# Front items of the expert stage: their tables, gathers and weight loads put some steps sooner and in the other order, and small tiles resized

## The chip, the cores and the metric

The kernel runs on one core of one Trainium2 chip. The metric is the time of one execution on the device in microseconds (us). Before the change it is 1503.58 us, the median of 3 runs (1500.83 to 1508.85).

## What is computed

Three stages in a row, all in float32. N = 4608 tokens (8 batches of 576), 512 channels (8 heads of 64).

```python
kv  = einsum('bhsd,bhse->bhde', k, v); o = einsum('bhsd,bhde->bhse', q, kv)
x   = o / sqrt(mean(o*o, -1) + 1e-6) * g_norm          # attention, (4608, 512)

logits = x @ w_gate + modality_bias[modality_id]       # 8 experts
e_idx  = argmax(logits); gate_w = softmax(logits)[e_idx]
x[mask_e] = gate_w * (relu(x[mask_e] @ w1[e]) @ w2[e]) # w1 512x1024, w2 1024x512

gate = sigmoid(x @ w_gate2); val = x @ w_val2          # 512 -> 1536
out  = (gate * val) @ w_out2                           # 1536 -> 512
```

With the inputs drawn, the experts 0 to 7 get 895, 331, 414, 770, 426, 483, 718 and 571 tokens; of the first half of the tokens they get 442, 187, 206, 364, 209, 236, 367 and 293.

## The kernel before

Precision comes from splitting each float32 operand into a high and a low part (suffix h and l): a product is three matmuls, high by high, high by low, low by high. ACT makes the high part, DVE the low part.

**Attention** is a loop over batches `for b in range(B + 1)` (line 638) with five steps r = 0 to 4 in each, one 128-token tile to a step; the output tile of batch b - 1 is made while batch b is prepared. DVE and POOL also route the tokens there: `norm` (L490 to L504) makes a batch's norms and logits, `choose` (L514 to L518) the expert, `rank` (L525 to L544) the token's place among its expert's, `lanes` (L551) and `numbers` (L561, L563) the tables that turn a place back into a token number. The order of each engine's instructions is the order of the code; no scheduler changes it.

**The expert stage** works on items. An item is a pair of 128-token tiles of one expert (late items a single tile). It has four steps; a step (t, j) multiplies by a quarter of w1 (`emit_B`, L266 to L268), applies relu and splits (`emit_h`, L280, L281), then multiplies by a quarter of w2 (`emit_D`, L313 to L315). Weights are loaded raw by SP (`load_w`, L190) in pieces of 512 KB, eight to an item, and split by ACT (L227) and DVE (L228). There are two raw buffers: half0, on the right of the memory, for the front items and the even items after them, and w1r1 with w2r1 for the odd ones. A piece is loaded under a flag: where the item's expert is that of the item before it in the same buffer, the transfer is skipped.

**Front items** 0 and 1 come from the first half of the tokens alone, which are routed while attention still runs. `front_items` (L579 to L604) sums the counts (matmul `tote`, L581) and chooses the two; `front_rows` (L606 to L617) makes their gather indices (`se` L611, matmuls `phe` L615, `gidx0` L617); POOL gathers their rows by indirect DMA (L208), SP reads their experts into registers (`read_item`, L167, L168), `norm_x` (L237) scales the rows and `emit_A` transposes (L245) and splits them (xh L249, xl L250). During the eight front steps the second half's routing is finished (`experts` L793 to L800, `places` L803 to L818). The front writes its result through `front.y` (`front_y`, L629) to y_d in memory.

**Items 2 to 21** run in `run`. Between their steps the third stage's weights are decoded from 64-bit floats (`Decode`: load L128, exponent on ACT L134, words and finish on DVE L140 to L149, store L155 to L157); the table `at` (L1024) says in which step s which unit is loaded, and exponent, words, finish and store come 2, 2, 3 and 4 steps after. `store_gate` (L1041, L1042) writes the gate values to memory for a later gather, `gate_t`, made in `number` (L894 to L898).

**The third stage** (GLU) follows: per step three matmuls by three (`gv`, L970 to L972), whose moving operand lies in half0, w1r1, w2r1 or other tiles and whose stationary one in a `wt` tile, and the output product (`ac`, L1335 to L1337; `wos` by `gh` and `gl`).

The change also touches the pool `oid` (bufs=3), from which `gate_t` comes. Tiles that are allocated after it lie behind it in memory.

Of the kernel before, what the change touches and what calls it, by code (L numbers as in the profile page):

```python
# [84 lines left out]
def attention_moe_glu_kernel(  # L85
# [249 lines left out]
    with ExitStack() as st:  # L335
# [243 lines left out]
        def front_items():  # L579
# [5 lines left out]
            ep = sm.tile([128, 4], F32, tag="ep", name="ep", bufs=1)  # L585
# [9 lines left out]
            nc.vector.tensor_tensor(out=le, in0=cue[3][:, 4:12].unsqueeze(1).broadcast_to(bc), in1=iota[:, 0:2].unsqueeze(2).broadcast_to(bc), op=ALU.is_le)  # L595
            nc.vector.tensor_reduce(out=ep[:, 0:2], in_=le, op=ALU.add, axis=AX)
            nc.vector.tensor_tensor(out=ep[:, 2:3], in0=ep[:, 1:2], in1=ep[:, 0:1], op=ALU.subtract)
# [3 lines left out]
            nc.vector.tensor_tensor(out=cd[:, 1:2], in0=cd[:, 1:2], in1=ep[:, 3:4], op=ALU.add)  # L601
# [25 lines left out]
        def front_y(i):  # L627
            if i == 0:
                front.y = wk.tile([128, 2, YW], F32, tag="qc", name="y", bufs=1)  # L629
            return front.y[:, i]  # L630
# [7 lines left out]
        for b in range(B + 1):  # L638
# [6 lines left out]
            for r in range(5):  # L645
                if b == B and r == 0:
                    ld_scope.close()
                    mw = [mw_scope.enter_context(tc.tile_pool(name="m_wr0", bufs=1, side="right", reuse_waits="tile"))]
                    w1p = w1_scope.enter_context(tc.tile_pool(name="m_w1", bufs=3, side="right", reuse_waits="tile"))
                    half0 = mw[0].tile([128, 2, KC * F1], F32, tag="half0", name="half0")  # L650
                    w1r.append(half0[:, 0].rearrange("p (c f) -> p c f", f=F1))
                    w2r.append(half0[:, 1].rearrange("p (c f) -> p c f", f=DM))
                    for j in range(NJ1):
                        load_w(0, j, 0)
                        load_w(0, j, 1)
                if b < B and r == 0:
                    nc.scalar.activation(out=qc[:, 1], in_=q_t[b][:, :, 1, :], func=ACTF.Copy)
                    for i in (2, 3):
                        nc.gpsimd.tensor_copy(out=qc[:, i], in_=q_t[b][:, :, i, :])
                if b:  # L660
                    emit_out(b - 1, r)
                if b < B:
                    if r == 0:
                        emit_RT(b)
                    if r < 4:
                        emit_qT((b, r), qc[:, r].rearrange("p h d -> p (h d)"))
                    elif b % 2:
                        emit_qT((b, 4), qr_t[b // 2].rearrange("p h d -> p (h d)"))
                    if r == 2:
                        emit_M(b)  # L670
                if r == 1:
                    load_kv(b + 2)
                    load_q(b + 2)
                    if b == 0:
                        load_mod()
                    if b > 1:
                        norm(b - 2)
                    for i in {5: (1,), 6: (0, 3, 2), 7: (4,)}.get(b, ()):
                        store_x(i)
                if b % 2 and b > 1:  # L680
                    if r == 3:
                        choose(b // 2 - 1)
                elif b > 2:
                    if r == 1:
                        lane = rank(b // 2 - 2)
                    elif r == 3:
                        lo = lanes(b // 2 - 2, lane)
                        if b < B:
                            numbers(b // 2 - 2, lo, False)
                if b == B - 2 and r == 2:  # L690
                    front_items()
                if b == B - 1:
                    if r == 2:
                        front_rows()
                    if r == 3:
                        for t in range(NFRONT):
                            gather(t)
                    if r == 4:
                        for t in range(NFRONT):
                            read_item(t)  # L700
                if b == B:
                    if r in (1, 2):
                        norm_x(0, r - 1)
                    if r in (2, 3):
                        emit_A(0, r - 2)
                    if r == 3:
# [85 lines left out]
        def experts():  # L792
# [4 lines left out]
            nc.vector.memset(esf[:, NITEM:NITEM + NFRONT + 2], 1.0)  # L797
            nc.vector.tensor_tensor(out=esf[:, NITEM + NFRONT + 2:2 * NITEM], in0=esf[:, NFRONT + 2:NITEM], in1=esf[:, NFRONT:NITEM - 2], op=ALU.not_equal)
# [91 lines left out]
    def number(b, i, src):  # L890
# [5 lines left out]
        if i == 0:  # L896
            gate_t[b] = oidp.tile([128, 2 * HT], F32, tag="gate", name="gate_t")
# [109 lines left out]
    with ExitStack() as st:  # L1007
# [498 lines left out]
```

## Time and profile before

| | us |
|---|---|
| median of 3 runs | 1503.58 |
| the profiled execution | 1505.5 |
| its span, first to last instruction | 1503.7 |
| PE busy in it | 1448.7 (96%) |
| DVE busy | 910.0 (61%) |
| ACT busy | 638.9 (42%) |
| POOL busy | 220.1 (15%) |
| mean granted TensorE clock, share of full | 0.987 |

PE is TensorE's matmuls, PEld its weight loads, DVE VectorE, ACT ScalarE, POOL GpSimd, SP the engine whose queue issues most transfers (SPq). In the page's 40 slices each digit is a share in tenths (9 is 90% or more). A wait is idle time of an engine, put down to what ended it. A matmul's duration overlaps the next one's, so busy time is not the sum of the durations.

### The profile page before, as it was taken

What the parts mean: (1) busy time and instruction counts of PE and PEld (TensorE: products, weight loads), DVE (VectorE), ACT (ScalarE), POOL (GpSimd) and SP (SyncE); (2) the same over time, 40 slices, a digit from 0 to 9 for tenths busy, and PEclk for the clock granted to TensorE, in tenths of its full rate; (3) what the DMA queues carried; (4) which work ended last, traced back from release to release, by engine and by line L of the source; (5) the groups of instructions that cost most, each with busy time, mean ns of one, the idle gap of its engine ahead of it and who ended that gap; (6) DMA issues with size and microseconds to landing.
All of it is one profiled execution on the core that took longest, in us unless ns stands there. A gap on an engine that the chain in (4) does not pass through costs nothing.

```text
span 1503.7 us, 22996 instructions
## 1 busy us (share of the span) xinstructions
PE 1448.7 (96%) x8670; PEld 1231.6 (82%) x8670; DVE 910.0 (61%) x1425; ACT 638.9 (42%) x1005; POOL 220.1 (15%) x304
## 2 busy tenths in 40 slices
PE   6986998999999999999999999999999999999997
PEld 6886887999999998778888887888888888888886
DVE  2566867888888887646866675343643436444342
ACT  3655644655555555745433342232322223221221
POOL 1012121222222212311011101020010200101001
PEclk9997999999999999999999999999999999999999
DMA  9984699988886757869886666556464654646444
GB/s 297 344 300 154 228 317 292 312 291 285 293 288 207 260 175 218 302 231 337 312 324 244 244 222 245 196 202 240 156 261 179 218 224 172 240 163 234 175 156 161
DMA packets 165154, 364.68 MB, mean 243 GB/s; under 512 B 21040, under 2 KB 82736, under 8 KB 157872
## 3 DMA queue, kind: packets, MB, share of 16 engines
q1 hardware_dynamic: 153104, 329.62, 63.4%
q0 software_dynamic: 10432, 32.08, 5.8%
q8 instruction: 70, 1.15, 0.3%
q10 hardware_dynamic: 1504, 1.48, 0.3%
q14 instruction: 44, 0.36, 0.1%
HBM read 302.88 MB, written 68.63 MB: 247 GB/s over the span
## 4 chain that ended last, share of the span: by engine, by line
PE 54%; DMA 4%; SPq 0%; issue 0%; POOL 0%; DVE 0%; ACT 0%; POOLq 0%; ACTq 0%
PE gv L970 10%; PE gv L972 10%; PE gv L971 10%; PE ac L1337 6%; PE ac L1335 6%; PE ac L1336 6%; DMA xg<-x_d,gidx 3%; PE gv L944 1%; PE gv L946 1%; PE gv L945 1%; PE tr L907 1%; DMA rows<-w_d 1%; DMA w_d<-d_f 0%; DMA y_d<-y,sidx 0%; SPq L1345 0%
## 5 line engine op out<-in xcount | busy, mean ns | idle before, releaser
L266 PE MATMUL ph<-xh,w1h 128*128 128x256 f32 x576 | 167.5, 291 | 5.6 <-ACT w1h L227 4.7
L974 DVE TENSOR_TENSOR gm<-u,gv 128x512 f32<-128x512 f32 x96 | 65.9, 686 | 176.4 <-PE gv L972 175.3
L267 PE MATMUL ph<-xh,w1l 128*128 128x256 f32 x576 | 165.8, 288 | 6.4 <-DVE w1l L228 6.4
L1337 PE MATMUL ac<-wos,gl 128*128 128x512 f32 x432 | 169.5, 392 | 0.0
L1335 PE MATMUL ac<-wos,gh 128*128 128x512 f32 x432 | 169.4, 392 | 0.0
L1336 PE MATMUL ac<-wos,gh 128*128 128x512 f32 x432 | 169.1, 391 | 0.0
L268 PE MATMUL ph<-xl,w1h 128*128 128x256 f32 x576 | 164.7, 286 | 0.4 <-DVE xl L250 0.4
L994 ACT ACTIVATE s<-gv 128x512 f32<-128x512 f32 x48 | 28.7, 599 | 268.7 <-issue 209.5
L267 PEld LDWEIGHTS ph<-xh,w1l 128*128 128x128 f32 x576 | 110.7, 192 | 9.5 <-DVE w1l L228 8.4
L266 PEld LDWEIGHTS ph<-xh,w1h 128*128 128x128 f32 x576 | 110.7, 192 | 8.2 <-ACT w1h L227 5.6
L970 PE MATMUL gv<-half,wt 128*128 128x512 f32 x288 | 114.3, 397 | 0.6 <-DVE u L974 0.6
L972 PE MATMUL gv<-half,wt 128*128 128x512 f32 x288 | 113.7, 395 | 0.0
L971 PE MATMUL gv<-half,wt 128*128 128x512 f32 x288 | 113.6, 394 | 0.0
L268 PEld LDWEIGHTS ph<-xl,w1h 128*128 128x128 f32 x576 | 110.8, 192 | 0.6 <-DVE xl L250 0.6
L313 PE MATMUL py<-w2h,hh 128*128 128x512 f32 x272 | 107.0, 393 | 0.0
L315 PE MATMUL py<-w2h,hl 128*128 128x512 f32 x272 | 106.7, 392 | 0.0
L314 PE MATMUL py<-w2l,hh 128*128 128x512 f32 x272 | 106.5, 392 | 0.0
L974 DVE TENSOR_TENSOR s<-u,gv 128x512 f32<-128x512 f32 x48 | 33.0, 688 | 121.2 <-PE gv L972 121.1
L1319 POOL DMA_INDIRECT out_dram<-ot,to x36 | 37.2, 1034 | 443.3 <-DVE ot L1316 191.6
L1337 PEld LDWEIGHTS ac<-wos,gl 128*128 128x128 f32 x432 | 81.1, 188 | 18.6 <-DVE gl L1304 0.4
L1336 PEld LDWEIGHTS ac<-wos,gh 128*128 128x128 f32 x432 | 81.1, 188 | 18.2
L1335 PEld LDWEIGHTS ac<-wos,gh 128*128 128x128 f32 x432 | 81.1, 188 | 18.2 <-ACT gh L1303 0.2
(305 smaller groups left out, 3370.3 us busy)
## 6 DMA issues: line engine op xcount, KB each, us to landing
wt<-wt_d SPq DMA_DIRECT2D x36, 1536.0 KB
half<-in_moe_w_dram SPq DMA_DIRECT2D x96, 512.0 KB
wos<-wo_d SPq DMA_DIRECT2D x96, 512.0 KB
w1r<-in_moe_w_dram SPq DMA_DIRECT2D x40, 512.0 KB
w2r<-in_moe_w_dram SPq DMA_DIRECT2D x40, 512.0 KB
rows<-w_d SPq DMA_DIRECT2D x24, 512.0 KB
wt<-wt_d SPq DMA_DIRECT2D x48, 256.0 KB
wt_d<-wt SPq DMA_DIRECT2D x12, 1024.0 KB
```

What stands on the lines that cost most here:

```text
L266: nc.tensor.matmul(out=o, lhsT=bh[:, c, cs], rhs=hi[:, c, 0:n], start=(c == 0), stop=False)
L267: nc.tensor.matmul(out=o, lhsT=bl[:, c, cs], rhs=hi[:, c, 0:n], start=False, stop=False)
L268: nc.tensor.matmul(out=o, lhsT=bh[:, c, cs], rhs=lo[:, c, 0:n], start=False, stop=(c == KC - 1))
L313: nc.tensor.matmul(out=o, lhsT=hi[:, f, cs], rhs=bh[:, f, :], start=first, stop=False)
L314: nc.tensor.matmul(out=o, lhsT=hi[:, f, cs], rhs=bl[:, f, :], start=False, stop=False)
L315: nc.tensor.matmul(out=o, lhsT=lo[:, f, cs], rhs=bh[:, f, :], start=False, stop=last)
L970: nc.tensor.matmul(out=o, lhsT=wh, rhs=yh[:, c, :], start=first and c == 0, stop=False, skip_group_check=True)
L971: nc.tensor.matmul(out=o, lhsT=wh, rhs=yl[:, c, :], start=False, stop=False, skip_group_check=True)
L972: nc.tensor.matmul(out=o, lhsT=wl, rhs=yh[:, c, :], start=False, stop=last and c == 1, skip_group_check=True)
L1335: nc.tensor.matmul(out=o, lhsT=gh[:, cs], rhs=wh, start=(k == 0), stop=False)
L1336: nc.tensor.matmul(out=o, lhsT=gh[:, cs], rhs=wl, start=False, stop=False)
L1337: nc.tensor.matmul(out=o, lhsT=gl[:, cs], rhs=wh, start=False, stop=(k == NJ - 1))
```

## The change

Four things are changed.

1. The front's pieces stand at other steps of the attention loop. At b = 6 the order is now rank (r = 0), lanes and numbers (1), norm (2), front_items (3); before it was norm and rank (1), front_items (2), lanes and numbers (3). At b = 7 the fifth query transpose, front_rows and the gathers stand at r = 0 (before 4, 2 and 3), the reading of the two experts and the eight loads of item 0 at r = 1 (before r = 4, and b = 8, r = 0). At b = 8, norm_x stands at r = 0 and 1 (before 1 and 2), emit_A at 3 and 4 (before 2 and 3), the first weight splits at r = 1, 2 and 4 (before 3, 4 and 4). In other batches norm comes behind rank.
2. The two front items change places: item 0 is the later expert, item 1 the earlier one. Item 2's flag is no longer the constant 1 but compares its expert with item 1's (L797, one DVE operation more).
3. `front.y` takes the tag "o1" in place of "qc", so that the first loads into w1r1 no longer overlap memory that the front's output is written from; `gate_t` has one buffer in place of three, which moves all tiles behind it down by 64 bytes: half0 stays at 96 modulo 128 bytes, while wt, w1r1, w2r1, gh and the w2 splits go from 32 to 96.
4. Decode's units start at step 13*i//6 + 3 in place of 9*i//4: the first three steps later, the last one later.

```diff
@@ front_items
-            nc.vector.tensor_tensor(out=le, in0=cue[3][:, 4:12].unsqueeze(1).broadcast_to(bc), in1=iota[:, 0:2].unsqueeze(2).broadcast_to(bc), op=ALU.is_le)
+            nc.vector.tensor_tensor(out=le, in0=cue[3][:, 4:12].unsqueeze(1).broadcast_to(bc), in1=ct[:, C_DESC + E - 2:C_DESC + E].unsqueeze(2).broadcast_to(bc), op=ALU.is_lt)
-            nc.vector.tensor_tensor(out=ep[:, 2:3], in0=ep[:, 1:2], in1=ep[:, 0:1], op=ALU.subtract)
+            nc.vector.tensor_tensor(out=ep[:, 2:3], in0=ep[:, 0:1], in1=ep[:, 1:2], op=ALU.subtract)
-            nc.vector.tensor_tensor(out=cd[:, 1:2], in0=cd[:, 1:2], in1=ep[:, 3:4], op=ALU.add)
+            nc.vector.tensor_tensor(out=cd[:, 0:1], in0=cd[:, 0:1], in1=ep[:, 3:4], op=ALU.add)
@@ front_y
-                front.y = wk.tile([128, 2, YW], F32, tag="qc", name="y", bufs=1)
+                front.y = wk.tile([128, 2, YW], F32, tag="o1", name="y", bufs=2)
@@ loop over b and r
-                if b == B and r == 0:
-                    ld_scope.close()
...
-                    for j in range(NJ1):
-                        load_w(0, j, 0)
-                        load_w(0, j, 1)
-                    elif b % 2:
+                    if b % 2 and r == (4 if b < B - 1 else 0):
                         emit_qT((b, 4), qr_t[b // 2].rearrange("p h d -> p (h d)"))
-                    if b > 1:
-                        norm(b - 2)
-                elif b > 2:
-                    if r == 1:
+                early = b == B - 2
+                if b > 2 and b % 2 == 0:
+                    if r == (0 if early else 1):
                         lane = rank(b // 2 - 2)
-                    elif r == 3:
+                    elif r == (1 if early else 3):
                         lo = lanes(b // 2 - 2, lane)
                         if b < B:
                             numbers(b // 2 - 2, lo, False)
-                if b == B - 2 and r == 2:
+                if b > 1 and r == (2 if early else 1):
+                    norm(b - 2)
+                if b % 2 and b > 1 and r == 3:
+                    choose(b // 2 - 1)
+                if early and r == 3:
                     front_items()
                 if b == B - 1:
-                    if r == 2:
+                    if r == 0:
                         front_rows()
-                    if r == 3:
                         for t in range(NFRONT):
                             gather(t)
-                    if r == 4:
+                    if r == 1:
                         for t in range(NFRONT):
                             read_item(t)
+                        ld_scope.close()
...
+                        for j in range(NJ1):
+                            load_w(0, j, 0)
+                            load_w(0, j, 1)
                 if b == B:
-                    if r in (1, 2):
-                        norm_x(0, r - 1)
-                    if r in (2, 3):
-                        emit_A(0, r - 2)
-                    if r == 3:
+                    if r in (0, 1):
+                        norm_x(0, r)
+                    if r in (3, 4):
+                        emit_A(0, r - 3)
+                    if r == 1:
                         split_w(0, 0, 0)
                         load_w(1, 0, 0)
+                    if r == 2:
+                        split_w(0, 0, 1)
+                        load_w(1, 0, 1)
                     if r == 4:
                         split_w(0, 1, 0)
                         load_w(1, 1, 0)
-                        split_w(0, 0, 1)
-                        load_w(1, 0, 1)
@@ experts
             nc.vector.memset(esf[:, NITEM:NITEM + NFRONT + 2], 1.0)
+            nc.vector.tensor_tensor(out=esf[:, NITEM + NFRONT:NITEM + NFRONT + 1], in0=esf[:, NFRONT:NFRONT + 1], in1=front.ep[0:1, 1:2], op=ALU.not_equal)
@@ number
-            gate_t[b] = oidp.tile([128, 2 * HT], F32, tag="gate", name="gate_t")
+            gate_t[b] = oidp.tile([128, 2 * HT], F32, tag="gate", name="gate_t", bufs=1)
@@ table at
-                at.setdefault((9 * i // 4 + d, what), []).append(i)
+                at.setdefault((13 * i // 6 + 3 + d, what), []).append(i)
```

Three places in the engines' orders show what moves. The first is DVE at b = 7, r = 0: R is the block of k-by-v products, rt its transposed copy, se, ve and gidx the front's index work.

```order
 L439 COPY R_150<-kv 64x4x64
 L440 COPY R_150<-kv 64x4x64
 L481 TENSOR_REDUCE ssq<-sq 128x8
 L449 COPY rt<-rtp 128x512
+L611 TENSOR_TENSOR se<-sce,code 128x72
+L616 TENSOR_SCALAR ve<-phe 128x4
+L617 TENSOR_TENSOR gidx_72<-ve,phe 128x4
 L481 TENSOR_REDUCE ssq<-sq 128x8
 L490 TENSOR_SCALAR ssq<-ssq 128x40
```

The three index operations, which stood behind norm(5) and the copy L456, now follow the copy L449 directly.

The second is DVE in the last round, b = 8: xg are the gathered rows, half the raw weights, w1l and w the low parts of a w1 and a w2 quarter. Ahead of rank (L525, L526), where norm(6) ended with L504:

```order
-L503 TENSOR_REDUCE lg<-uo 128x32
-L504 TENSOR_TENSOR lg<-lg,bias 128x32
+L481 TENSOR_REDUCE ssq<-sq 128x8
+L237 TENSOR_TENSOR xg<-xg 128x4x128
+L481 TENSOR_REDUCE ssq<-sq 128x8
 L525 TENSOR_REDUCE tr<-oh 128x8
 L526 TENSOR_TENSOR tot<-tot,tr 128x8
```

And behind rank:

```order
+L503 TENSOR_REDUCE lg<-uo 128x32
+L504 TENSOR_TENSOR lg<-lg,bias 128x32
+L237 TENSOR_TENSOR xg<-xg 128x4x128
+L228 TENSOR_TENSOR w1l<-half_1776,w1h 128x1024
+L481 TENSOR_REDUCE ssq<-sq 128x8
+L228 TENSOR_TENSOR w_1905<-half_1776,w_1905 128x1024
 L481 TENSOR_REDUCE ssq<-sq 128x8
 L551 TENSOR_TENSOR lo<-iotab,lane 128x1152
 L250 SCALAR_TENSOR_TENSOR xl<-xtp,gcol,xh 128x4x128
```

The first scaling L237 now stands ahead of rank, norm(6) behind it; the second scaling and two weight splits stand ahead of lanes (L551), where before the splits came last.

The third is SP's queue where item 2's last piece and item 3's first ones are issued; the names in brackets are the semaphores that each waits for (DMASW those of POOL's transfers). Before:

```order
L190 DMA half_1821<-in_moe_w_dram 128x2x512 [waits DMAHW1_49,DVE_49]
L190 ISA
L190 DMA w1r_2711<-in_moe_w_dram 128x4x256 [waits DMASW3_49,DMASW2_49,DMASW4_49,DVE_49,DMASW5_49,PE_49,DMAHW2_49,Activation_49,Pool_49]
L190 ISA
L190 DMA w1r_2711<-in_moe_w_dram 128x4x256 [waits DMAHW3_49]
```

And now:

```order
L190 DMA half_1776<-in_moe_w_dram 128x2x512 [waits DMAHW1_49,DVE_49]
L190 ISA
L190 DMA w1r_2712<-in_moe_w_dram 128x4x256 [waits DMAHW2_49,DVE_49,PE_49]
L190 ISA
L190 DMA w1r_2712<-in_moe_w_dram 128x4x256 [waits DMAHW3_49]
```

The first load into w1r1 no longer waits for POOL, its transfers or ACT; it still waits for DVE and PE.

## Rows read from the trace of the kernel before

**Rows 1.** The page's 40 slices of the span: granted TensorE clock in tenths.
```profile
PEclk9997999999999999999999999999999999999999
```
**Rows 2.** Waits of PE, 85 to 150 us: engine, line, releaser: total us, times, longest.
```profile
PE xtp L245 <- DVE xg L237: 6.1, 1, 6.1
...
PE phe L615 <- DVE se L611: 3.4, 1, 3.4
PE ph L267 <- DVE w1l L228: 1.9, 1, 1.9
PE tote L581 <- DVE tot L526: 1.9, 1, 1.9
```
**Rows 3.** Window: us, then busy us (count) of PE, PEld, DVE, ACT, POOL; clock, DMA share, GB/s.
```profile
129.80:148.00 18.20, 9.88 (x66) 8.82 (x65) 12.65 (x35) 9.95 (x17) 1.51 (x3) 0.77 0.86 280
```
**Rows 4.** Timeline of DVE: start us, duration us, instruction, in brackets idle time before it.
```profile
118.83 0.69 DVE L449 COPY rt<-rtp 128x512 f32<-128x512 f32 x1
...
124.31 0.22 DVE L611 TENSOR_TENSOR se<-sce,code 128x72 bf16<-128x72 bf16 x1
125.75 0.16 DVE L616 TENSOR_SCALAR ve<-phe 128x4 f32<-128x4 f32 x1 [1.21 <-PE phe L615]
...
132.78 0.69 DVE L481 TENSOR_REDUCE ssq<-sq 128x8 f32<-128x512 f32 x1 [1.67 <-ACT sq L480]
...
141.71 0.75 DVE L250 SCALAR_TENSOR_TENSOR xl<-xtp,gcol,xh 128x512 fp32r<-128x512 f32 x1 [0.73 <-ACT xh L249]
...
146.78 1.22 DVE L228 TENSOR_TENSOR w1l<-half,w1h 128x1024 fp32r<-128x1024 f32 x1
```
**Rows 5.** Timeline of POOL: the first gather.
```profile
126.40 1.18 POOL L208 DMA_INDIRECT xg<-x_d,gidx  x1 [3.00 <-DVE gidx L617]
```
**Rows 6.** The tile xg, 80 to 300 us: from a gather's issue to its landing.
```profile
DMA to landing us min/median/max: 3.6/5.6/8.2
```
**Rows 7.** Timeline of SP's queue at three places (x8: eight issues).
```profile
129.78 20.35 SPq L190 DMA_DIRECT2D half<-in_moe_w_dram  x10
...
191.57 7.64 SPq L190 DMA_DIRECT2D half<-in_moe_w_dram  x8
...
223.93 3.02 SPq L1042 DMA_DIRECT2D gate_d<-gate  x1
```
**Rows 8.** Waits of SP's queue, 85 to 260 us.
```profile
SPq L190 <- PE qps L461: 15.5, 1, 15.5
...
SPq L190 <- DMA y_d<-y: 9.5, 1, 9.5
```
**Rows 9.** Timeline of DVE: the last operation of places().
```profile
206.58 0.26 DVE L818 TENSOR_SCALAR sidx<-v,ct 128x44 int32<-128x44 f32 x1
```
**Rows 10.** Waits, 200 to 300 us.
```profile
ACT d_e L134 <- DMA d_raw<-in_moe_w_gate_dram: 11.3, 2, 6.6
...
PE ph L266 <- ACT w1h L227: 4.3, 2, 3.4
PE ph L267 <- DVE w1l L228: 4.1, 3, 1.5
```
**Rows 11.** Window behind those waits, columns as in rows 3.
```profile
229.00:238.00 9.00, 7.28 (x31) 6.71 (x32) 6.88 (x10) 4.07 (x6) 0.00 (x0) 0.62 0.78 64
```
**Rows 12.** Groups of PE by shape: count, busy us, mean ns of one, idle us before.
```profile
L970 PE MATMUL gv<-half,wt 128*128 128x512 f32 x288 | 114.3, 397 | 0.6 <-DVE u L974 0.6
L971 PE MATMUL gv<-half,wt 128*128 128x512 f32 x288 | 113.6, 394 | 0.0
L970 PE MATMUL gv<-w1r,wt 128*128 128x512 f32 x168 | 66.7, 397 | 0.0
L971 PE MATMUL gv<-w1r,wt 128*128 128x512 f32 x168 | 65.4, 389 | 0.0
L1335 PE MATMUL ac<-wos,gh 128*128 128x512 f32 x432 | 169.4, 392 | 0.0
```
**Rows 13.** Timeline of SP's queue later on: one issue whose transfer is skipped.
```profile
468.84 0.10 SPq L190 DMA_DIRECT2D w1r<-in_moe_w_dram  x1
```

More of the change, by code (lines that the diff above doesn't have):

```diff
@@ L584, in front_items @@
             le = sm.tile([128, 2, 8], F32, tag="le", name="le", bufs=1)
-            ep = sm.tile([128, 4], F32, tag="ep", name="ep", bufs=1)
+            ep = front.ep = sm.tile([128, 4], F32, tag="ep", name="ep", bufs=1)
             cd = sm.tile([128, 2], F32, tag="cd", name="cd", bufs=1)
@@ L645, in attention_moe_glu_kernel @@
             for r in range(5):
-                if b == B and r == 0:
-                    ld_scope.close()
[L648 to L652, printed above, removed]
-                    for j in range(NJ1):
-                        load_w(0, j, 0)
-                        load_w(0, j, 1)
                 if b < B and r == 0:
@@ L675, in attention_moe_glu_kernel @@
                         load_mod()
-                    if b > 1:
-                        norm(b - 2)
                     for i in {5: (1,), 6: (0, 3, 2), 7: (4,)}.get(b, ()):
                         store_x(i)
-                if b % 2 and b > 1:
-                    if r == 3:
-                        choose(b // 2 - 1)
-                elif b > 2:
-                    if r == 1:
+                early = b == B - 2
+                if b > 2 and b % 2 == 0:
+                    if r == (0 if early else 1):
                         lane = rank(b // 2 - 2)
-                    elif r == 3:
+                    elif r == (1 if early else 3):
                         lo = lanes(b // 2 - 2, lane)
@@ L689, in attention_moe_glu_kernel @@
                             numbers(b // 2 - 2, lo, False)
-                if b == B - 2 and r == 2:
+                if b > 1 and r == (2 if early else 1):
[3 more added lines that the diff above has]
+                if early and r == 3:
                     front_items()
                 if b == B - 1:
-                    if r == 2:
+                    if r == 0:
                         front_rows()
-                    if r == 3:
                         for t in range(NFRONT):
                             gather(t)
-                    if r == 4:
+                    if r == 1:
                         for t in range(NFRONT):
                             read_item(t)
-                if b == B:
-                    if r in (1, 2):
-                        norm_x(0, r - 1)
-                    if r in (2, 3):
-                        emit_A(0, r - 2)
-                    if r == 3:
+                        ld_scope.close()
+                        mw = [mw_scope.enter_context(tc.tile_pool(name="m_wr0", bufs=1, side="right", reuse_waits="tile"))]
+                        w1p = w1_scope.enter_context(tc.tile_pool(name="m_w1", bufs=3, side="right", reuse_waits="tile"))
+                        half0 = mw[0].tile([128, 2, KC * F1], F32, tag="half0", name="half0")
+                        w1r.append(half0[:, 0].rearrange("p (c f) -> p c f", f=F1))
+                        w2r.append(half0[:, 1].rearrange("p (c f) -> p c f", f=DM))
+                        for j in range(NJ1):
+                            load_w(0, j, 0)
+                            load_w(0, j, 1)
+                if b == B:
+                    if r in (0, 1):
[3 more added lines that the diff above has]
+                    if r == 1:
                         split_w(0, 0, 0)
                         load_w(1, 0, 0)
+                    if r == 2:
+                        split_w(0, 0, 1)
+                        load_w(1, 0, 1)
                     if r == 4:
```

## The prediction

> **What bounds the kernel now.** I read the page first, for the busy shares and the clock by slices, then PE's waits by window, then the engine that ends each wait. PE is 1448.7 us busy of a span of 1503.7, so only some 55 us can be won without making matmuls shorter. The clock by slices [rows 1] lies at full speed everywhere but in the first slices, so PE's idle time is in the attention stage and the front: what there is to win stands before 260 us. Behind that, the kernel is a stream of matmuls whose own pace decides.
>
> Between 85 and 150 us PE waits 6.1 us for the scaled rows, 3.4 for se, 1.9 for the first w1l and 1.9 for tot [rows 2]. All four are ended by DVE. The same stretch shows that DVE is not simply full: from 129.8 to the end of the first w1l split (146.78 + 1.22 = 148.0 [rows 4]) it works 12.65 us of 18.20 [rows 3] and stands idle for 5.55, because the items of its queue are in an order in which the first ones wait for ACT and PE. The second loss is between 200 and 260 us. There ACT waits 11.3 us for d_raw with a w1h split queued behind the exponent, and PE waits 4.3 us for w1h and 4.1 for w1l [rows 10]. Behind it the clock is 0.62 for 9 us [rows 11].
>
> **The sum, term 1: the front's lead.** The order is DVE's, so each wait is taken by itself.
> (a) The tote matmul now stands three steps behind the rank that makes tot; before it stood one step behind. Its wait of 1.9 us goes. What covers it is two steps of attention; were the cover gone, the 1.9 would be back.
> (b) se moves from 124.31 to directly behind the copy L449 at 118.83 [rows 4]. PE comes to phe just behind the transposes that L449 reads, so it now waits for 0.69 (L449) and 0.22 (se), with the handing over some 1.2 by my estimate. The wait of 3.4 falls by 2.2.
> (c) Now DVE waits for phe with work of attention behind it. It waited 1.21 us for it before [rows 4], at a place where PE's next work did not hang on it. I take the whole 1.2 off.
> (d) In the last round the scalings and two weight splits go into the idle 5.55 us. Two waits of 0.73 us, of L250 for ACT's xh [rows 4], stay. What can be filled is 5.55 - 1.5 = 4.1. From this I hold back 1.0 for waits on ACT's squares, of which the largest is 1.67 [rows 4].
> Together: 1.9 + 2.2 - 1.2 + 4.1 - 1.0 = 6.0 us.
>
> For (d) the data must be there. The first gather is issued at 126.40 [rows 5], 2.1 us behind se. With (a), se comes at 118.83 + 0.69 - 1.9 = 117.6, the gather at 119.7, and the slowest landing of 8.2 us [rows 6] puts it at 128; DVE comes to the first scaling, whose place is just ahead of the row at 132.78 and moves up by at most 4, about then or a little later. The weights are not late: item 0's loads start at 129.78 [rows 7] after SP has waited 15.5 us [rows 8] for the last transposed query of attention, whose source lies in the memory that ld_scope frees; that transpose moves from b = 7, r = 4 to r = 0, so the loads start near 117 (beside se), 13 us sooner, and a weight is wanted only near 133. In SP's queue nothing of attention stands behind them but stores of x_d for the second half, which only later gathers read; the four moved gathers read the first half alone, whose stores stand ahead. On POOL they move ahead of norm(5)'s copy L501, a short one.
>
> I expect the sum to carry through to item 2, since the next long waits of PE are those of rows 10 (term 2). Bounds: below 2.9 ((d) gives nothing: 1.9 + 2.2 - 1.2), above 10 (all of 6.1 + 1.9 + 1.9 of rows 2, as if the front had no wait).
>
> **Term 2: the step from item 2 to item 4.** Item 2's expert is expert 0, which is item 1's in the new order, so its eight transfers of 512 KB are skipped. Before they were issued from 191.57 for 7.64 us [rows 7]; a skipped issue takes 0.10 us [rows 13]. The first load into w1r1 waited 9.5 us for y_d [rows 8]; this semaphore is gone, but it still waits for DVE, whose places() ends at 206.58 [rows 9]. So it comes about 2 us sooner, and with term 1's lead 8. Decode's first load comes three steps later, which takes the exponents out of ACT's queue while item 3's weights are split: the 11.3 us of ACT's wait [rows 10] fall away there. With them go PE's waits: 4.3 + 4.1, less 1.1 that I leave for the one w1l that no d_raw stands ahead of, is 7.3. The low clock goes with the wait: the matmuls of that window, 7.28 us busy at 0.62 [rows 11], need 7.28 × 0.38 = 2.8 us less at the full one. Sum 10.1. I hold back 2 us, because d_raw's first load now comes behind the gate stores; one of these takes 3.02 us [rows 7] to issue and in the window after them only 64 GB/s move [rows 11], so a late d_raw can still block ACT once. Term 2 is 8. Bounds: 3 (the w1h wait alone goes, and half of it comes back elsewhere) and 10.1.
>
> **Term 3: alignment.** No row shows why two tiles that differ by 64 bytes modulo 128 should matter; the nearest rows are the means of the same product with the moving operand in half0 (96 modulo 128 against wt's 32) and in w1r1 (32 against 32): 397 and 397 ns for L970, 394 and 389 for L971 [rows 12]. The difference is 0 to 5 ns. The matmuls with half0 are 3 × 288 and 3 × 88 of the first products, 1128; taking the middle, 1128 × 2.5 ns = 2.8 us. Bounds 0 and 5.6. The output product has wos at 96 and gh at 32, and its 392 ns [rows 12] lie with the better group, so I give nothing for it.
> The Trainium skill ("SBUF — State Buffer", section "SBUF: two separate sides") says that on the engines' side only the pair of ports that GpSimd and VectorE share causes contention and that PE's port waits on nobody; by that, alignment would change nothing, and the sum would be 14.0 in place of 16.8. The 5 ns of L971 speak against it weakly, the 0 ns of L970 for it.
>
> **Nothing for the rest.** The added DVE operation (L797) works on one number, like the index operations of rows 4 at some 0.2 us, beside PE's work of a front step; without that cover it costs its 0.2. The swap of the two items changes no count of matmuls: both are full pairs. Decode's last load comes one step later; it is far from its reader, since a unit is stored four steps on.
>
> **Sum.** 6.0 + 8.0 + 2.8 = 16.8 us. The profiled execution took 1505.5, so 1488.7; it lies 1.9 above the median of the runs, so the median to expect is 1486.8, say **1487 us**, 1.1% less.
>
> **Rivals.**
> A, the forecast: 1487, chance 0.55.
> B, the second stall comes back. d_raw stands behind the gate stores, ACT waits for it in step 5 as it did before, and PE goes low once more. For it: the 64 GB/s [rows 11]. Against: the exponent comes two steps after the load, and that window is only 9 us long. Term 2 is then 3: 1503.6 - 11.8 = 1492, chance 0.20.
> C, alignment does nothing: 1503.6 - 14.0 = 1490, chance 0.12. For it the equal 397 ns [rows 12]. The rule of the Trainium skill given above is this case.
> D, the front is blocked in DVE. DVE's queue is in order; if the first scaling waits for its gather, rank waits behind it, then tot and all of the second half's routing. For it: landing takes up to 8.2 us [rows 6] and the margin is near zero. Term 1 is then 2.9 and the rest stays: 1503.6 - 13.7 = 1490, chance 0.08.
> F, the change does not do what it says: item 2's flag is 1 after all (its expert is not item 1's), so the eight loads go out, and with 4 MB ahead of w1r1's the w1h wait stays as it was (3.4 of rows 10): 1503.6 - 13.4 = 1490, chance 0.03.
> E, slower: equal residues hurt. In the products with half0 and in the output product (1128 + 3 × 432 = 2424 matmuls) both operands now agree modulo 128; if two streams read from like addresses got in each other's way, a matmul would take longer. From 14.0 / 2424 = 5.8 ns it eats the other gains, at 9 ns (2424 × 9 = 21.8) it makes the kernel 1503.6 + 7.8 = 1511 us. Against: w1r1 with wt agree already and are not slower [rows 12]. Chance 0.02.
>
> **How the numbers follow.** The chances are the mixture of these: B, C, D and F lie within 6 us of the forecast, and the bounds of the terms that are least known (2 held back in term 2, 2.8 either way in term 3, 3.1 below and 4 above in term 1) do not all go one way. The lower end takes half of them: 2 + 2.8 + 4 = 8.8 below, 1479 rounded; the upper end takes the case that two of the rivals hold together (B and C, or B and D, 5 each): 1497. What a measurement can tell from no change is 0.5%, 7.5 us: 1496.1 and 1511.1. Faster 0.89, same 0.09 (two rivals together with a small term 1, or more), slower 0.02 (E).
>
> **What would show it.** In the profile after: no wait of tote for tot, phe's near 1 us, gathers from about 120, half0's loads from about 117, the first dense product 6 us sooner; no eight half0 transfers ahead of w1r1's; no wait of ACT for d_raw ahead of a w1h split, and the window behind 225 us at full clock; means of L970 to L972 with half 2 or 3 ns less. The forecast is wrong if PE's waits before 260 us fall by less than 8 us, if a new wait stands at the first scaling or at d_raw, or if the third stage changes by more than 6 us.

## The result, and the profile after

The changed kernel takes 1494.6 us (median of 6 runs, 1492.35 to 1496.6), the one before 1507.66 beside it (median of 6, 1500.83 to 1510.15). The ratio is 0.9919, 95% interval 0.9895 to 0.9944: 0.8% or 12 us faster. Against the 1503.58 us that the forecast started from, this ratio is 1491.4 us; forecast were 1487, and 1492 for its rival B. The profiled execution took 1492.35 us.

The page of the changed kernel: span, busy times, and the queue of SP's transfers (packets, MB, share).

```profile
span 1490.6 us, 22989 instructions
...
PE 1440.0 (97%) x8670; PEld 1225.9 (82%) x8670; DVE 912.4 (61%) x1426; ACT 638.6 (43%) x1005; POOL 221.0 (15%) x304
...
q1 hardware_dynamic: 149904, 325.42, 63.2%
```

The transfers are 4.2 MB less than before (329.62 MB): item 2's eight pieces are skipped, so the change does what it says.

To see where the time went, the span is cut at three starts read from PE's timeline: the k-by-v product of b = 7, the first product of item 2, and the first product of the third stage (L944). Windows between them, columns as in [rows 3]; first the kernel before:

```profile
85.00:111.10 26.10, 20.34 (x260) 18.91 (x258) 14.72 (x54) 12.85 (x24) 1.57 (x4) 0.87 0.92 347
111.10:202.90 91.80, 77.69 (x708) 70.42 (x706) 67.06 (x158) 52.70 (x100) 16.68 (x20) 0.91 0.62 204
...
202.90:653.20 450.30, 439.17 (x2785) 390.34 (x2785) 354.55 (x458) 264.10 (x363) 100.84 (x111) 0.99 0.80 263
...
653.20:1496.20 843.00, 840.33 (x3704) 683.46 (x3704) 436.97 (x663) 262.70 (x439) 84.72 (x133) 1.00 0.62 227
```

The same stretches of the changed kernel:

```profile
85.00:108.10 23.10, 19.27 (x251) 17.96 (x250) 14.31 (x36) 12.04 (x23) 5.45 (x5) 0.85 0.87 325
108.10:195.30 87.20, 73.95 (x708) 65.95 (x706) 69.15 (x175) 52.66 (x101) 12.84 (x20) 0.94 0.55 192
...
195.30:643.10 447.80, 438.40 (x2784) 390.55 (x2785) 354.36 (x458) 264.33 (x363) 101.81 (x111) 0.99 0.81 262
...
643.10:1483.00 839.90, 837.82 (x3704) 683.51 (x3704) 436.98 (x663) 262.39 (x438) 84.60 (x133) 1.00 0.62 228
```

Up to item 2 the changed kernel is 7.6 us ahead (202.9 to 195.3). From there to the third stage it wins 2.5 more, and in the third stage, with as many matmuls, 3.1. These sum to 13.2; the spans differ by 13.1. The forecast's terms for these were 6.0, 8.0 and 2.8: the second is the one that failed.

PE's waits of the changed kernel from 85 to 150 us answer to [rows 2]:

```profile
PE qps L461 <- ACT qT L463: 3.1, 1, 3.1
PE ops L475 <- ACT o L477: 2.6, 1, 2.6
PE ph L266 <- ACT xh L249: 2.5, 1, 2.5
PE ph L268 <- DVE xl L250: 2.2, 1, 2.2
PE ops L475 <- DVE R L456: 1.8, 1, 1.8
PE rtp L447 <- DVE R L440: 1.3, 1, 1.3
PE rkp L528 <- DVE oh L518: 0.8, 2, 0.5
...
PE xtp L245 <- DVE xg L237: 0.3, 1, 0.3
```

The 1.9 of tote and the 3.4 of phe's wait for se are gone, the 6.1 of xtp is 0.3. But six waits that were not there, or were shorter, stand in their place. One of them, the 3.1 of qps, takes the place of kv's 3.7 (now 0.7) and is not the change's: two other kernels with the new loop (gap ahead of gh, item 2 loaded, below) have 4.3 at kv and none at qps. With two small ones between them all of PE's waits in this stretch sum to 15.5 us; before, with 3.7 for kv and two small ones beside [rows 2], it was 17.6.

DVE and POOL answer to [rows 4] and [rows 5]. DVE's timeline of the changed kernel:

```profile
104.57 1.58 DVE L490 TENSOR_SCALAR ssq<-ssq 128x32 f32<-128x32 f32 x1
106.84 1.40 DVE L493 TENSOR_TENSOR tt<-rsq 128x32 f32<-128x32 f32 x1
...
116.41 0.22 DVE L611 TENSOR_TENSOR se<-sce,code 128x72 bf16<-128x72 bf16 x1
117.87 0.16 DVE L616 TENSOR_SCALAR ve<-phe 128x4 f32<-128x4 f32 x1 [1.24 <-PE phe L615]
```

And POOL's:

```profile
104.00 4.18 POOL L563 TENSOR_TENSOR lid<-lo,tokb 128x1152 bf16<-128x1152 bf16 x2 [15.73 <-DVE lo L551]
...
118.52 1.18 POOL L208 DMA_INDIRECT xg<-x_d,gidx  x1 [7.88 <-DVE gidx L617]
```

se and the first gather come about 8 us sooner, 1.2 ahead of the forecast (117.6 and 119.7). L490 and L493 take 1.6 and 1.4 us beside POOL's two L563, and each ends within 0.1 us of one of these (106.15 and 108.24; 106.11 and 108.18). At their seven other places in this profile they take 0.2.

The second loss is there again, later and once. PE's waits from 200 to 300 us of the changed kernel, for [rows 10]:

```profile
PE ph L266 <- ACT w1h L227: 3.2, 1, 3.2
PE ph L267 <- DVE w1l L228: 2.7, 2, 1.6
```

What ends them, on ACT's timeline:

```profile
237.53 0.66 ACT L134 ACTIVATE d_e<-d_raw 128x512 f32<-128x512 f32 x1 [6.83 <-DMA d_raw<-in_moe_w_gate_dram]
```

The window behind, for [rows 11], has the clock at 0.62 as before:

```profile
239.00:248.00 9.00, 7.24 (x30) 6.71 (x31) 7.57 (x10) 4.63 (x8) 0.00 (x0) 0.62 1.05 382
```

And SP's queue ahead of that load:

```profile
213.19 0.70 SPq L1041 DMA_DIRECT2D gate_d<-gate  x1
213.94 1.70 SPq L1042 DMA_DIRECT2D gate_d<-gate  x1
215.68 1.49 SPq L1041 DMA_DIRECT2D gate_d<-gate  x1
217.21 2.19 SPq L1042 DMA_DIRECT2D gate_d<-gate  x1
219.74 6.84 SPq L190 DMA_DIRECT2D half<-in_moe_w_dram  x4
226.75 0.84 SPq L128 DMA_DIRECT2D d_raw<-in_moe_w_gate_dram  x1
```

Last, the groups of [rows 12]. The products with half shown here have fallen by 3 to 4 ns each; the output product, which was to stay, has risen by 3:

```profile
L1335 PE MATMUL ac<-wos,gh 128*128 128x512 f32 x432 | 170.5, 395 | 0.0
...
L970 PE MATMUL gv<-half,wt 128*128 128x512 f32 x288 | 113.1, 393 | 0.7 <-DVE u L974 0.7
L971 PE MATMUL gv<-half,wt 128*128 128x512 f32 x288 | 112.5, 391 | 0.0
...
L970 PE MATMUL gv<-w1r,wt 128*128 128x512 f32 x168 | 66.1, 394 | 0.0
L971 PE MATMUL gv<-w1r,wt 128*128 128x512 f32 x168 | 65.6, 390 | 0.0
```

### The profile page after: what moved, and what is told of

The parts are those of the page before. It is cut to its first block, busy times and chain, and to the rows that moved or that the text cites. A ratio compares the mean times of both kernels' runs of the same rounds, so it can differ in the third digit from the quotient of the medians.

```text
span 1490.6 us, 22989 instructions
## 1 busy us (share of the span) xinstructions
PE 1440.0 (97%) x8670; PEld 1225.9 (82%) x8670; DVE 912.4 (61%) x1426; ACT 638.6 (43%) x1005; POOL 221.0 (15%) x304
## 4 chain that ended last, share of the span: by engine, by line
PE 86%; DMA 7%; DVE 3%; issue 1%; ACT 1%; SPq 1%; POOL 0%; POOLq 0%; ACTq 0%; DVEq 0%
PE gv L970 10%; PE gv L971 10%; PE gv L972 10%; PE ac L1337 7%; PE ac L1335 7%; PE ac L1336 7%; PE ph L267 5%; PE ph L268 4%; PE ph L266 4%; PE py L314 4%; PE py L315 4%; PE py L313 4%; DMA xg<-x_d,gidx 3%; DMA vt<-in_v_dram 1%; PE ops L475 1%
## 5 line engine op out<-in xcount | busy, mean ns | idle before, releaser
L970 PE MATMUL gv<-half,wt 128*128 128x512 f32 x288 | 113.1, 393 | 0.7 <-DVE u L974 0.7
L971 PE MATMUL gv<-half,wt 128*128 128x512 f32 x288 | 112.5, 391 | 0.0
L972 PE MATMUL gv<-half,wt 128*128 128x512 f32 x288 | 112.4, 390 | 0.0
```

The source lines that it names most:

```text
L970: nc.tensor.matmul(out=o, lhsT=wh, rhs=yh[:, c, :], start=first and c == 0, stop=False, skip_group_check=True)
L971: nc.tensor.matmul(out=o, lhsT=wh, rhs=yl[:, c, :], start=False, stop=False, skip_group_check=True)
L972: nc.tensor.matmul(out=o, lhsT=wl, rhs=yh[:, c, :], start=False, stop=last and c == 1, skip_group_check=True)
```

## The experiments

Each kernel is the changed one with one edit, or the one before with one part of the change. The table has the median of the runs, the ratio to the kernel before on the same chip with its 95% interval, and the time of item 2's start and the two later stretches (item 2 to the third stage, third stage) in each profile, read as above. The medians come from several chips, on which the kernel before had 1505.14 to 1510.26 us, so a difference of two medians holds to a few us only; where it matters, the difference of the two ratios is given beside it.

| kernel | us | ratio | item 2 starts | to third stage | third stage |
|---|---|---|---|---|---|
| before | 1507.66 | 1 | 202.9 | 450.3 | 843.0 |
| changed | 1494.6 | 0.9919 (0.9895 to 0.9944) | 195.3 | 447.8 | 839.9 |
| before, gate_t in one buffer | 1503.53 | 0.9981 (0.9966 to 0.9996) | 204.8 | 452.6 | 844.1 |
| gate_t in three buffers | 1498.27 | 0.9952 (0.9935 to 0.9969) | 194.5 | 448.9 | 842.6 |
| gap ahead of gh | 1487.78 | 0.9878 (0.9859 to 0.9898) | 199.4 | 448.5 | 834.9 |
| old loop | 1500.63 | 0.9968 (0.9949 to 0.9988) | 198.7 | 448.5 | 841.9 |
| item 2 loaded | 1498.06 | 0.9949 (0.9924 to 0.9973) | 198.9 | 447.9 | 842.2 |
| old Decode table | 1497.29 | 0.9948 (0.9926 to 0.9969) | 195.2 | 450.2 | 840.3 |
| gate stores late | 1488.9 | 0.9894 (0.9854 to 0.9934) | 198.7 | 439.8 | 842.5 |
| exponent a step later | 1487.71 | 0.9885 (0.9857 to 0.9912) | 198.6 | 440.5 | 842.2 |
| gap, exponent later | 1481.02 | 0.9809 (0.9779 to 0.984) | 199.4 | 440.0 | 837.3 |
| the same, old loop | 1486.48 | 0.9851 (0.9819 to 0.9883) | 203.6 | 440.3 | 833.2 |
| the same, other order at b = 6 | 1480.74 | 0.9807 (0.9777 to 0.9837) | 196.1 | 440.3 | 835.1 |
| the same, y under its old tag | 1479.96 | 0.9828 (0.9804 to 0.9852) | 198.1 | 441.3 | 834.7 |

In nine of these profiles the clock falls once near the third stage's start (0.94 to 0.97 in the window of 640 to 700 us, where the other five have 1.00), kernels of every kind among them, which costs 2 to 4 us by estimate (0.03 to 0.06 of the 60); the third stage is therefore compared among the five that have no such fall: before, changed, gate_t in three buffers, old Decode table, and gap with the old loop.

**Addresses.** In the changed kernel half0 stands at 224 modulo 256 bytes and wt, w1r1, w2r1, gh and gl at 224 too, where before those stood at 32; wos stands at 96 in both. The first run makes this move of 64 bytes alone, in the kernel before:

```diff
-            gate_t[b] = oidp.tile([128, 2 * HT], F32, tag="gate", name="gate_t")
+            gate_t[b] = oidp.tile([128, 2 * HT], F32, tag="gate", name="gate_t", bufs=1)
```

> The kernel before with gate_t in one buffer: all small tiles behind it move down by 64 bytes, nothing else changes. Theory A (each matmul's pace hangs on both operands' addresses modulo 256: quickest where they agree, slowest where they agree modulo 128 alone): gv<-half falls from 394-397 ns to 390-393, gv<-w1r and gv<-w2r by 1-2 ns, ac<-wos rises from 392 to 395; the sum is -3 us, 0.2%. Theory B (agreeing modulo 128 is enough, as the forecast had it): gv<-half falls alike, ac stays at 392; -5 us. Theory C (addresses do nothing, the means differ between the two kernels for another cause): all means as in the kernel before, 0 us.

Measured: gv<-half 393, 391 and 390 ns (L970 to L972), ac<-wos 395, 395 and 394; 0.9981. These are theory A's means. B falls with the output product's rise, C with all of them. The time, 0.6 to 5.1 us less by the interval, fits A's 3 and does not exclude B's 5.

The reverse edit on the changed kernel:

> The changed kernel with gate_t back in three buffers. Theory A: the means go back to those of the kernel before (gv<-half 394-397 ns, ac 392), the time is 3 us above the changed kernel. Theory B: 5 us above. Theory C: the means stay at 390-393 and 395, no difference.

The means go back (gv<-half 397, 394 and 395, ac 392), and the third stage with them: 842.6 us in place of 839.9, as before 843.0. That is theory A again, by the means; the time, 3.7 us more by the medians and 5.0 by the ratios, does not tell A from B.

Then the addresses are made to agree modulo 256 in the output product also:

```diff
+        ws.tile([128, 32], F32, name="gap", bufs=1)
         for t in ("gh", "gl"):
             ws.tile([128, HC], F32R, tag=t, name=t)
```

> The changed kernel with 128 bytes left free ahead of gh and gl: they go from 224 to 96 modulo 256, where wos stands, and agree modulo 128 as before. Theory A: ac falls from 395 ns to about 390, gv stays; 1296 x 5 ns = 6 us below the changed kernel. Theory B: they agreed already, no difference. Theory C: no difference.

The output product's group in that kernel (its lines are one further down):

```profile
L1336 PE MATMUL ac<-wos,gh 128*128 128x512 f32 x432 | 168.7, 390 | 0.0
```

390 ns in place of 395, and 6.8 us less by the medians, 6.2 by the ratios: A. Its operand addresses (96 for wos) were 64 apart modulo 256 in the kernel before, 392 ns, 128 apart in the changed one, 395, and are equal here, 390. The third stage took 833.2 us with the gap (old loop) and 839.9 without.

**Between item 2 and the third stage.** Three edits, each undoing one thing. The first leaves out L797, so that item 2 is loaded:

> The changed kernel with item 2's flag at 1, so its eight weight pieces are loaded again though half0 holds them. Theory A (the skip is what keeps DMA free ahead of item 3's weights): 4 MB more at 200 to 205 us, item 3's first weights land some 10 us later, PE waits for w1h at item 3's first step, 3 to 8 us above the changed kernel. Rival (DMA had room there, and places() sets when item 3's loads start): same time within 2 us.

The stretch is 447.9 us against 447.8, the wait for w1h 3.4 against 3.2. Item 3's loads start 4.1 us behind item 2's start in both (202.97 and 198.9; 199.38 and 195.3). The rival: the skip is worth nothing in this stretch. The median is 3.5 us higher, with intervals that overlap, which alone would fit theory A. But the profile's difference lies ahead of item 2's start (198.9 against 195.3), within what this start spreads over among kernels with the same loop (194.5 to 199.4). Whether the eight transfers, issued from 187.62 us on, have a part in it is not shown.

```diff
-                at.setdefault((13 * i // 6 + 3 + d, what), []).append(i)
+                at.setdefault((9 * i // 4 + d, what), []).append(i)
```

> The changed kernel with Decode's old table. Theory A (the later start of Decode is worth what the two stalls before became one): two waits of ACT for d_raw again, PE's waits for w1h and w1l 7 us in place of 4.8, time 2 to 5 us above the changed kernel. Rival (with item 2's loads skipped the first d_raw comes in time, in an emptier queue): no stall at all, 5 to 8 us below the changed kernel.

PE's waits of that kernel from 200 to 300 us:

```profile
PE ph L266 <- ACT w1h L227: 4.3, 2, 3.0
PE ph L267 <- DVE w1l L228: 4.1, 3, 1.5
```

These totals are those of [rows 10], and the stretch is 450.2, as before: theory A. So 2.4 of the 2.5 us of the changed kernel are the Decode table's.

```diff
-                if not s and sure:
+                if s == 12 and sure:
                     store_gate()
```

> The changed kernel with the gate stores moved from step 0 of run to step 12, away from the first d_raw load. Theory A (the many small packets of the gate stores hold back the queues, so d_raw takes 11 us to land): the wait of ACT for d_raw at 237 us goes, with PE's 4.8 us and the half clock behind it, worth 3; 7 to 8 us below the changed kernel. Rival (d_raw is late behind the weights that were issued ahead of it, 2 MB in 7 us, gate stores or not): the wait stays, no difference.

SP's queue of that kernel, without the stores ahead of d_raw:

```profile
212.30 10.63 SPq L190 DMA_DIRECT2D half<-in_moe_w_dram  x7
223.10 0.58 SPq L128 DMA_DIRECT2D d_raw<-in_moe_w_gate_dram  x1
```

And its only wait of PE from 200 to 300 us that the view lists:

```profile
PE ph L267 <- DVE w1l L228: 1.1, 1, 1.1
```

Theory A: the waits and the low clock (1.00 from 215 to 240 us) are gone, 8.0 us in the stretch; the medians differ by 5.7, with intervals that overlap. Its mechanism is only half shown. Counted from item 2's start, d_raw is issued after 31.5 us in the changed kernel (226.75 less 195.3) and after 24.4 here (223.10 less 198.7): it is 7.1 us later because SP issues the gate stores ahead of it for 6.2 us (213.19 to 219.40). Whether it also lands faster cannot be told, as nobody waits for it here. Nor are the gate stores the only thing that makes d_raw late. In the kernel before, SP issues its first load ahead of them, behind item 3's eight loads:

```profile
215.36 0.46 SPq L128 DMA_DIRECT2D d_raw<-in_moe_w_gate_dram  x1
```

And ACT waits for it all the same:

```profile
227.54 0.66 ACT L134 ACTIVATE d_e<-d_raw 128x512 f32<-128x512 f32 x1 [6.58 <-DMA d_raw<-in_moe_w_gate_dram]
```

From the issue to the exponent that waited for it 12.2 us pass there, 13.1 at the second stall (behind the gate stores) and 10.8 in the changed kernel (237.53 less 226.75). What is common to the three is that the load is issued too few us ahead of its reader, whatever holds it up.

```diff
-            for d, what in ((0, "load"), (2, "exponent"), (2, "words"), (3, "finish"), (4, "store")):
+            for d, what in ((0, "load"), (3, "exponent"), (3, "words"), (4, "finish"), (5, "store")):
```

> The changed kernel with Decode's exponent, words, finish and store one step later behind the load (3, 3, 4, 5). Under both readings of why d_raw is late the wait of 6.8 us shrinks to 1 or less, since a step takes 6 us: PE's 4.8 us and the half clock behind it, worth 3, go; 6 to 8 us below the changed kernel. If instead another wait takes their place (ACT held by the next weights' landing), less than 3 below.

ACT's wait for d_raw is 1.5 us (1 or less was expected), PE has none from it, and the stretch is 440.5. The six profiles without the stall have 439.8 to 441.3 us in this stretch, the five with the stall and the changed table 447.8 to 448.9. Two edits of different kinds thus put the stall at 7.3 to 8.0 us: 4.8 of PE's waiting in the changed kernel (3.2, and 1.6 of the 2.7) and the rest low clock.

**Together.** The gap and the later exponent in one kernel:

> The changed kernel with both the 128 bytes ahead of gh and gl and Decode's exponent one step later. Theory (the two are independent: one shortens the output products, the other removes the wait of ACT for d_raw): the gains add, 6 and 7 us, 13 below the changed kernel, ratio to the kernel before near 0.983. Rival (one takes what the other gave, as where the stage after absorbs a lead): 7 below, ratio 0.988.

1481.02 us and 0.9809, 13.6 us below the changed kernel by the medians: the gains add. This version beats both kernels, by 1.9% and 0.9%.

**The front.** The loop over b and r as it was before, all else as changed:

```diff
                 if b == B - 1:
-                    if r == 0:
+                    if r == 2:
                         front_rows()
...
-                    if r == 1:
+                    if r == 4:
                         for t in range(NFRONT):
                             read_item(t)
...
```

> The changed kernel with the attention loop's old order (front pieces at their old steps), all else as changed. Theory A (the lead carries through): item 2's first product waits end near 202 us in place of 195, the four waits of PE for DVE at tote, phe, xtp and w1l are back, time 7 to 8 us above the changed kernel. Rival (the lead is swallowed by the stall at item 3's weights, whose end DMA sets): that stall gets shorter by as much as the lead is lost, time 0 to 3 us above.

The four waits are back (tote 0.7 this time, phe 3.2, xtp 6.1, w1l 1.9), and the kernel is 6.0 us slower by the medians, 7.4 by the ratios. The stretch behind item 2 is 448.5 against 447.8: the stall there does not swallow the lead. Item 2 starts at 198.7 in this profile, 4 us sooner than in the kernel before with the same loop, so one profile does not measure the lead. It was measured again where nothing else stalls (the run ahead, in the next texts, is the kernel with gap and later exponent):

> The kernel of the run ahead with the attention loop's old order. Nothing behind the front is left that could swallow a lead, so the difference is the lead itself. Theory A (the forecast's term 1): 6 us slower than the run ahead. Theory B (the new order pays back a part: front_items' sixteen operations stand ahead of the R copies on DVE and PE waits for those, and two operations of norm run into POOL's): 2 to 4 us slower.

1486.48 against 1481.02: 5.5 us, though the two intervals overlap. Item 2 starts at 198.7 to 204.8 in the four profiles with the old loop, mean 202.5, and at 194.5 to 199.4 in the nine with the change's, mean 197.6: 4.9 us. Cut at the first k-by-v products of b = 6 and b = 7, 2.8 of the 4.9 lie in the round b = 6 (22.48 and 19.65 us on average) and 2.0 between there and item 2 (91.62 and 89.61). In that last part the four old ones lie between 91.5 and 91.7 and the nine new ones between 87.1 and 91.4, so the changed kernel's own profile, 87.2, is one of the two best. Theory A is nearer. But B's payback is there too, and this run asks what it costs:

```diff
+                    elif r == (2 if early else 3):
+                        if early:
+                            front_items()
                         lo = lanes(b // 2 - 2, lane)
...
+                if b > 1 and r == 1:
                     norm(b - 2)
```

> The kernel of the run before last with another order at b = 6: norm at r = 1, front_items and behind it lanes and numbers at r = 2. Theory B says that norm's operations L490 and L493 fall from 1.58 and 1.40 us to 0.2 since POOL's L563 no longer runs beside them, that PE's wait of rtp for the R copies (1.3 to 4.2 us) goes, and that the time is 2 to 4 us below. Rival (that wait is one of several in a row, the next one, of ops or xtp, takes it over): L490 and L493 are short, PE's waits between 85 and 150 us sum to the same, no difference.

DVE's timeline of it at b = 6:

```profile
102.30 0.17 DVE L490 TENSOR_SCALAR ssq<-ssq 128x32 f32<-128x32 f32 x1
103.16 0.19 DVE L493 TENSOR_TENSOR tt<-rsq 128x32 f32<-128x32 f32 x1
```

PE's waits from 85 to 150 us:

```profile
PE qps L461 <- ACT qT L463: 4.2, 1, 4.2
PE ops L475 <- ACT o L477: 3.2, 1, 3.2
PE ph L266 <- ACT xh L249: 2.5, 1, 2.5
PE ph L268 <- DVE xl L250: 2.2, 1, 2.2
PE phe L615 <- DVE se L611: 1.8, 1, 1.8
PE ops L475 <- DVE R L456: 1.3, 1, 1.3
PE kv L438 <- issue: 0.7, 1, 0.7
```

The operations are short and rtp's wait (3.0 in the kernel it is compared with) is gone, yet the waits sum to 15.9 us in both, and the medians are the same (1480.74 and 1481.02): the rival. Item 2 starts 3.3 us sooner in this profile, but the one that it is compared with is that of the slowest of that kernel's five executions. At this place a wait that goes is taken over by the next.

**The tag of y.** Last, on the kernel with gap and later exponent, front.y under its old tag:

> The kernel of the quickest pair (gap ahead of gh and gl, exponent one step later) with front.y back under its old tag, so that item 3's first loads wait for the stores of y again. Theory A (places() holds those loads nearly as long, and the loads have slack before ACT wants them): the wait of SP for y_d is back, the loads start 2 to 5 us later, PE has no new wait, same time. Rival (the loads are what item 3's first step waits for once d_raw is out of the way): PE waits for w1h again at item 3, 3 to 8 us slower.

SP waits 8.8 us for y_d again, but the loads start at 202.81, 4.7 us behind item 2's start, against 4.1 without it: places() holds them nearly as long. PE waits for w1l 2.3 us in place of 1.1 and not for w1h. The median is 1.1 us lower and the ratio 2.9 us higher, with intervals that overlap: theory A, though a loss of up to 3 us is not excluded.

## Why the prediction was right, and where it was not

The direction and the range held; the size was forecast at 1.1% and measured at 0.8%. Of the cases the forecast's own (1487) did not come, and rival B (1492, given 0.20) did, at its place and with its price. Two of the forecast's three signs of being wrong came with it: PE's waits before 260 us fell by 4.9 us (42.6 to 37.7) and not by 8, and a wait stands at d_raw. The lower end of its range is 1478 by its own sum (1487 less 8.8), not 1479, which changes nothing here.

- **Term 1, 6.0 us: right in size, in part by luck.** By runs it is 5.5 to 6.0 (6.3 to 7.4 by the ratios). (a) tote's wait is gone. (b) phe no longer waits for se in this profile (0.9 in the one with the old Decode table). (c) DVE waits 1.24 us for phe, and PE then 1.8 for R: forecast 1.2. (d) failed as it was put. The idle time of DVE was filled, but PE did not get it as less waiting: from b = 7 on PE stands idle 13.3 us (87.20 less 73.95) where it stood 14.1 (91.80 less 77.69). What it did get in this profile is 3.7 us less busy time at a clock of 0.94 in place of 0.91; over all profiles it is 2.3 us less busy time and as much idle time (14.5 and 14.2). So (b), (c) and (d), together forecast at 4.1 us from b = 7 on, came to 2.0. The waits were spread over more places, behind each other in ACT's and DVE's queues. The forecast took the sum of DVE's idle time for PE's gain, and it missed that the moved work has a price on DVE: front_items' eighteen operations (L587 to L604) directly ahead of the R copies, and two of norm beside POOL's L563. In the round ahead of b = 7 the gain is more than the 1.9 of (a): 2.8 us over all profiles, 1.7 of it idle time.
- **Term 2, 8.0 us: wrong, 2.5.** The step that failed is "the 11.3 us of ACT's wait fall away there". By the table the first exponent moves from step 2 to step 5, which is still among item 3's steps: on ACT it stands directly ahead of item 3's last w1h split (237.53 and 238.09), and ACT waits 6.8 us. The size of the whole stall was right: taken away, it gives 10.5 (450.3 less 439.8), forecast 10.1. But the first d_raw was only put three steps later, which is behind the gate stores in SP's queue, and ACT wants it two steps after the load in either table, as it did in the kernel before, where it was late ahead of them. The forecast saw the gate stores, and held back 2 us for a load "that can still block ACT once"; once is all it takes for PE's wait and the low clock, 7 to 8 us. Two contributors that it named, the skipped loads and the freed y_d wait, were worth nothing that the stretch shows, for the reason that it gave itself: places() holds item 3's loads.
- **Term 3, 2.8 us: right in size by luck, for a sum of two parts that it did not have.** The products with half fell by 3 to 6 ns (L970 to L972, L944 to L946), the upper end. The output product, to which it gave nothing, rose by 3 ns. That is the mechanism of rival E, priced there for the products with half also; it ate about half of the gain. The step that failed is agreeing modulo 128: the output product agreed modulo 128 with and without the gap, and took 390 and 395 ns. The Trainium skill ("SBUF — State Buffer", section "SBUF: two separate sides") says that TensorE's port waits on nobody, from which the forecast had it that no address would matter. The output product's 390 and 395 ns in kernels that differ by a gap alone go against that conclusion, and the measurement decides; whether PE waits on another engine there no run shows.
- **Rival C** falls with that; **D** too: the first scaling came at 128.11 and xtp waited 0.3 us. **F**: the page's 4.2 MB less show that the flag takes.

## What to carry to other kernels

Before a load is moved to a later step, write down what its queue issues ahead of it there, and what waits in order behind its reader: the same stall comes back if the distance from load to reader stays the same. Idle time of an engine that feeds the bottleneck is not the bottleneck's gain; count the waits that come next in the two queues, and confirm the sum with an experiment that undoes the move. After any change of a tile's size compare the mean time of every large matmul group: a gap of 128 bytes was worth about as much here as the whole reordering of the front (6.2 to 6.8 us, and 5.5 to 7.4).

## What was not expected of the hardware

- The pace of these matmuls hangs on their operands' addresses in the memory, and that they agree modulo 128 bytes is not enough. Modulo 256 bytes, with both equal (96 for ac with the gap, 224 for gv<-half as changed) the means are 390 to 391 ns, L970 apart, which has 393. With ac's 64 apart they are 391 to 392, with ac's 128 apart 394 to 395, and with gv<-half's at 224 and 32 they were 394 to 397. Equal at 32 (w1r with wt before) they were 389 to 397 by line, equal at 224 390 to 394. That 256 bytes is the period, and that the distance alone counts, is not shown, as few addresses were tried; why it is so stays open.
- A DVE operation on 32 elements a partition took 1.58 and one 1.40 us beside POOL's elementwise L563, and 0.17 and 0.19 once L563 had been moved away. The Trainium skill ("SBUF — State Buffer", section "SBUF: two separate sides") calls the port pair that the two engines share an exclusive lock for the whole instruction; the numbers agree, as the two operations end with POOL's, and the second run shows that moving them apart removes the loss.
- Between the old and the new front, PE's gain from b = 7 on came as clock and not as idle time: 0.91 in all four profiles of the old one, 0.91 to 0.94 in the nine of the new one, with as much idle time. The granted clock has to be read beside the waits.
